# An FFT-style convolution on one core: steady tiles as two 64-row TensorE streams, and the last two frequencies inverted from on-chip memory

## The chip, the cores and the metric

The kernel runs on one core of a Trainium2 chip. The core has five engines that run side by side: TensorE (matmul), VectorE, ScalarE, GpSimd and SyncE, and 16 DMA engines. Operands lie in on-chip memory with 128 partitions; TensorE writes into eight accumulation banks (PSUM), from which VectorE and ScalarE read. The metric is the device time of one execution in microseconds. In the profile PE is TensorE's matmuls, PEld its weight loads, DVE is VectorE, ACT is ScalarE, POOL is GpSimd and SP is SyncE; a "q" behind a name is that engine's instruction queue.

## The reference

A circular 7 x 7 convolution of a 224 x 224 image with 96 channels in and 96 out, written with two-dimensional transforms:

```python
wp = jnp.pad(w, ((0, H - K), (0, W - K), (0, 0), (0, 0)))
Xf = rfft2(x, axes=(1, 2)); Wf = rfft2(wp, axes=(0, 1))
Yf = jnp.einsum('bhwi,hwio->bhwo', Xf, Wf)
y = irfft2(Yf, s=(H, W), axes=(1, 2)).astype(jnp.bfloat16)
```

Input and output are bf16; x is 1 x 224 x 224 x 96, w is 7 x 7 x 96 x 96.

## The kernel before

The kernel transforms only along the image's height, in eight bands of 28 output rows (with 6 rows more, a length of 34, so 17 frequencies s = 0 to 16). Along the width it uses the seven taps directly, with a fast scheme that computes two neighbouring columns at once: three products per pair (m = 0, 1, 2, with 4, 4 and 3 taps; `TAPS`). A complex product takes three real ones (three "parts"). For s > 0 that is 3 x 4 + 3 + 4 matmuls into a first bank and 2 x (3 + 4) into a second, 33 in all, and 22 for s = 0. Each has 96 rows of contraction (the channels), 128 columns of weights (16 column pairs by 8 bands) and 96 moving columns (output channels).

The width is cut into seven tiles of 32 columns (t = 0 to 6). A tile has these stages:

- A (`a_jobs`, line 395): forward transform; TensorE multiplies x, loaded into the four `xn` buffers, by the table `Fm`; ScalarE or VectorE moves the banks into `xf`. `evac` (line 115) gives each bank to the engine with the smaller running cost.
- J (`jit`, line 418): VectorE makes sums and differences of `xf` for groups of three frequencies (`JGB`), three instructions each, a burst that is handed to `b_round` as `planes`.
- B (`b_round`, line 446): the 33 matmuls against the transformed weights `WF`. ScalarE scales one part, VectorE forms u and v, and the sum u + v goes to `yf`: by GpSimd, or by VectorE (`ydve`) in a round that carries a burst.
- Frequencies go out of `yf` to a scratch buffer in DRAM (`scr`), three at a time (`YGRP`), and come back transposed as `tt` (`load_t`, line 537).
- C (`c_jobs`, line 568): inverse transform with the table `Gm` over three groups of bands, 24 matmuls of 384 columns a tile, moved to `yo` and out.

The order of each engine's instructions is that in which the program issues them[...]. Two tiles are worked first, t = 0 with t = 1 four rounds behind (`LAG`), while the weight transform (`prep_jobs`) is woven in; A of tile 2 runs in the last four rounds. Then tiles 2 to 6 follow one another. In each, A of the next tile and C of the two tiles before are woven between the rounds by `pace`. All loads and stores, but for a few at the end, are issued by SyncE in program order, each with its waits. The last tile writes its frequencies in three parts (0 to 8, 9 to 14, 15 and 16) to scratch; at the end the inverse adds one matmul with `GA` (the first part) and one with `GB` (the rest) per bank, and 36 matmuls on a zero tile (`WARM`) stand between them.

The profile names almost every operation by the one line of a helper (L84), so groups are told apart by tiles and shapes.

## Time and profile before

| | |
|---|---|
| time, three runs | 298.6, 299.13 (median), 299.9 us |
| span of the profiled execution | 298.6 us |
| what lies outside its span, against the median | 0.5 us |
| mean granted TensorE clock | 0.964 |
| busy: PE, PEld, DVE, ACT, POOL | 271.7, 243.5, 237.5, 197.8, 87.0 us |
| DMA moved | 46.01 MB, mean 154 GB/s |
| one B matmul (PE, mean) | 207 ns |
| one sum on GpSimd, on VectorE (mean) | 1006, 586 ns |

A matmul's 207 ns is from its start to its modelled end; they overlap, so PE counts as busy when one is under way, and the rate is read from starts. The chain is the sequence of work that ended last, followed back from the last instruction. A window's row gives, for a stretch of the span, the busy time and number of instructions of each engine, the granted clock (1.00 is full), the share of the DMA engines and their rate.

### The profile page before, as it was taken

What the parts mean: (1) busy time and instruction counts of PE and PEld (TensorE: products, weight loads), DVE (VectorE), ACT (ScalarE), POOL (GpSimd) and SP (SyncE); (2) the same over time, 40 slices, a digit from 0 to 9 for tenths busy, and PEclk for the clock granted to TensorE, in tenths of its full rate; (3) what the DMA queues carried; (4) which work ended last, traced back from release to release, by engine and by line L of the source; (5) the groups of instructions that cost most, each with busy time, mean ns of one, the idle gap of its engine ahead of it and who ended that gap; (6) DMA issues with size and microseconds to landing.
All of it is one profiled execution on the core that took longest, in us unless ns stands there. A gap on an engine that the chain in (4) does not pass through costs nothing.

```text
span 298.6 us, 11728 instructions
## 1 busy us (share of the span) xinstructions
PE 271.7 (91%) x4882; PEld 243.5 (82%) x4882; DVE 237.5 (80%) x508; ACT 197.8 (66%) x494; POOL 87.0 (29%) x124
## 2 busy tenths in 40 slices
PE   8488998988888886999999999999999999999992
PEld 3377987978887776989889989798998989788961
DVE  7846399999999948686988879876998889867823
ACT  2445995746452484888578886888789875676313
POOL 6810011222224421234152233234143223342100
PEclk9955999999999998999999999999999999999999
DMA  8894142111111357977847686687828643778765
GB/s 185 141 223 123 49 114 77 44 42 42 43 43 42 111 169 174 213 221 202 233 119 203 195 238 190 195 229 202 240 76 208 203 139 116 197 177 232 201 131 184
DMA packets 45828, 46.01 MB, mean 154 GB/s; under 512 B 33626, under 2 KB 34758, under 8 KB 45678
## 3 DMA queue, kind: packets, MB, share of 16 engines
q1 hardware_dynamic: 43488, 43.21, 54.3%
q10 hardware_dynamic: 2288, 2.06, 2.4%
q8 instruction: 38, 0.62, 0.9%
q14 instruction: 14, 0.11, 0.1%
HBM read 23.92 MB, written 21.33 MB: 152 GB/s over the span
## 4 chain that ended last, share of the span: by engine, by line
PE 59%; DVE 22%; DMA 7%; ACT 5%; issue 4%; SPq 1%; DVEq 0%; ACTq 0%
PE pb L84 59%; DVE J L84 7%; DVE v L84 5%; DMA wq<-in_w_dram 4%; DVE yf L84 3%; ACT WF L84 3%; DVE u L84 2%; DVE WF L84 2%; DVE xf L84 2%; DMA xf<-scrb 1%; ACT xf L84 1%; DMA xn<-in_x_dram 1%; SPq L84 1%; DMA scrb<-yf 1%; ACT yo L84 0%
## 5 line engine op out<-in xcount | busy, mean ns | idle before, releaser
L84 PE MATMUL pb<-WF,J 96*128 96x96 bf16 x2898 | 169.3, 207 | 7.9 <-DVE J L84 7.9
L84 PEld LDWEIGHTS <-J 96*128 96x128 bf16 (+1 forms) x2910 | 143.5, 98 | 24.2 <-DVE J L84 9.1
L84 POOL TENSOR_TENSOR yf<-v,u 128x384 bf16<-128x384 f32 x74 | 73.8, 1006 | 177.7 <-issue 103.2
L84 ACT CAST xf<-pb 96x408 bf16<-96x408 f32 (+1 forms) x153 | 67.3, 485 | 12.9 <-PE pb L84 10.1
L84 ACT CAST yo<-pb 84x384 bf16<-84x384 f32 (+1 forms) x144 | 61.3, 480 | 7.1 <-PE pb L84 4.1
L84 PE MATMUL pb<-WF,xf 96*128 96x96 bf16 x952 | 61.2, 207 | 4.4 <-DVE WF L84 4.3
L84 DVE TENSOR_TENSOR J<-xf 96x1824 bf16<-96x1824 bf16 (+1 forms) x84 | 57.4, 722 | 0.0
L84 PEld LDWEIGHTS <-xf 96*128 96x128 bf16 x952 | 47.8, 98 | 5.0 <-issue 4.2
L84 PE MATMUL pb<-Fm,xn 118*128 118x136 bf16 x448 | 50.0, 232 | 2.1 <-DVE u L84 1.5
L84 PE MATMUL pb<-tt,Gm 102*84 102x384 bf16 (+1 forms) x144 | 36.2, 329 | 1.1 <-DVE u L84 0.5
L84 ACT CAST WF<-pb 96x480 bf16<-96x480 f32 (+1 forms) x65 | 32.8, 587 | 6.0 <-PE pb L84 5.9
L84 PEld LDWEIGHTS <-xn 118*128 118x128 bf16 x448 | 31.8, 102 | 3.8 <-issue 2.9
L84 PE MATMUL pb<-wq 98*128 98x120 bf16 (+1 forms) x336 | 26.6, 232 | 3.5 <-DMA wq<-in_w_dram 3.5
L84 PEld LDWEIGHTS <-wq 98*128 98x128 bf16 (+1 forms) x336 | 23.6, 151 | 4.9 <-POOL ct L84 3.6
L84 DVE TENSOR_TENSOR J<-J 96x912 bf16<-96x912 bf16 (+1 forms) x42 | 25.0, 595 | 0.0
L84 DVE TENSOR_TENSOR yf<-v,u 128x384 bf16<-128x384 f32 x38 | 22.2, 586 | 1.3
L84 DVE TENSOR_TENSOR WF<-WF 96x480 bf16<-96x480 bf16 x30 | 18.7, 629 | 2.9 <-ACT WF L84 2.8
L84 PEld LDWEIGHTS <-Gm 102*84 102x84 bf16 (+1 forms) x144 | 11.5, 114 | 3.5 <-issue 0.8
L84 PE MATMUL pb<-wu 128*112 128x384 bf16 (+1 forms) x60 | 12.7, 374 | 1.1 <-DVE ct L84 1.1
L84 PEld LDWEIGHTS <-wu 128*112 128x112 bf16 (+1 forms) x60 | 7.3, 123 | 6.0 <-issue 2.1
L84 DVE CAST xf<-pb 96x408 bf16<-96x408 f32 (+1 forms) x19 | 8.9, 512 | 1.3 <-PE pb L84 1.3
L84 ACT CAST tt<-pb 112x384 bf16<-112x384 f32 x8 | 3.6, 479 | 9.2 <-PE pb L84 9.1
(388 smaller groups left out, 207.6 us busy)
## 6 DMA issues: line engine op xcount, KB each, us to landing
xn<-in_x_dram SPq DMA_DIRECT2D x28, 336.0 KB
scr<-yf SPq DMA_DIRECT2D x30, 288.0 KB
tt<-scr SPq DMA_DIRECT2D x24, 288.0 KB
out_dram<-yo SPq DMA_DIRECT2D x24, 252.0 KB
tt<-scr SPq DMA_DIRECT2D x12, 192.0 KB
out_dram<-yo SPq DMA_DIRECT2D x12, 168.0 KB
out_dram<-tt SPq DMA_DIRECT2D x4, 336.0 KB
scr<-yf SPq DMA_DIRECT2D x6, 192.0 KB
```

The costliest lines, as they stand in the source:

```text
L84: r = fn(*a, **k)
```

## The change

In tiles 2 to 6 the 96 channels no longer fill one 96-row matmul. TensorE's rows are used as two halves of 64, by `tile_position`. The lower half ("lo") takes channels 0 to 63, one matmul per tap. The upper half ("hi") holds channels 64 to 95 twice, the second time shifted by two taps, so one matmul does two taps; it also takes two of the three parts of m = 0 for channels 0 to 63, so that both halves have 25 or 26 matmuls a frequency. `t_round` issues them in turn, hi some 20 matmuls behind (`step8`, `FLUSH`); both add into the same bank, and before a bank's first hi matmul `row_wait` holds TensorE's queue until the last lo matmul is done. A (`f_jobs`) and C are split into 64-row halves in the same way; C now spans four bands with 512 columns, and frequency 16 goes through a small table `GR`.

The layout is made by copies on chip: `shift` copies channels 64 to 95 of `xf` to partitions 96 to 127 once per tile, `bring` copies channels 0 to 63 to partitions 64 to 127 per group of three frequencies, and `convert` rearranges `WF` once, group by group as tile 1 leaves it. All three are issued by SyncE. The weight transform's taps are put in the order of `TPOS` by ten small GpSimd copies. From tile 2 on all sums but the last three of tile 6 run on GpSimd and no longer wait for the burst; the halo copy of `xf` moves from VectorE to GpSimd. PSUM is split into 5 banks for B and 3 for the rest, `YBUF` goes from 4 to 3, and J keeps three buffers throughout. A of tile 2 is split: frequencies 0 to 7 four rounds earlier, the others in the last four rounds; its planes are made after the last round.

At the end frequencies 15 and 16 of the last tile stay in `yf`: `direct` adds them to the banks with 128 matmuls of 32 rows and 192 columns against the table `SG`, which `d_job` fills; `WARM` goes from 36 to 8, and the output goes in eight stores in place of four.

```diff
+TPOS = {7: 0, 8: 1, 2: 2, 0: 3, 1: 4, 3: 5, 9: 6, 6: 7, 4: 8, 5: 9}
...
+ND = 2 * (17 - 15)
 YMAX = 3
-YBUF = 4
+YBUF = 3
 JGB = ((0, 3), (3, 6), (6, 9), (9, 12), (12, 15), (15, 17))
 LAG = 4
-CQ = {2: (12, 0), 3: (12, 2), 4: (10, 5), 5: (7, 8), 6: (4, 12)}
-NXN = 4
-NP2 = 0
-WARM = 36
+CQ = {2: (6, 0), 3: (6, 0), 4: (6, 0), 5: (6, 0), 6: (6, 6)}
+SH = 8
+FLUSH = 20
+WARM = 8
...
+    def load_x(t, jg):
+        load_rows(xn_bufs[jg], jg, t * 2 * TW, 2 * PXC)
...
+    mo = ftile([PW2, NTAP])
+    for tap, pos in TPOS.items():
+        GE.tensor_copy(out=mo[:, pos:pos + 1], in_=mk[:, tap:tap + 1])
...
+    def d_job(a, g):
+        k = a * NJ + 4 * g
+        VE.tensor_tensor(out=SG[:, a, g].rearrange("p q (j m) -> p q j m", j=4), in0=Gv[:].unsqueeze(2).to_broadcast([128, ND, 4, B]),
+                         in1=Gk[:, k:k + 4].unsqueeze(1).unsqueeze(3).to_broadcast([128, ND, 4, B]), op=ALU.mult)
...
+                o, i = (v[0:C, ph, :, s0:s1, p:p + HALO, :].rearrange("c r s w j -> c r s (w j)") for v, p in ((xf, 0), (prev, TW)))
+                apart(("A", t), ("halo", s0), (VE if t < 2 else GE).tensor_copy(out=o, in_=i))
...
+    def f_jobs(t, part, jgs, tiled, load):
+        s0, s1 = ((0, SH), (SH, NS))[part]
+        n = 2 * (s1 - s0) * JG
+        runs = ((0, 8), (8, 16)) if part == 0 else ((0, 6), (6, 11), (11, 16))
+        fv = Fm[:, :, s0:s1].rearrange("p r s j -> p r (s j)")
+        jobs = []
+
+        def mk_(jg, a, b, last):
+            xb = xn_bufs[jg]
+            m = b - a
+            st = {}
+
+            def mm(ph, k, h, start=True, stop=True):
+                i = 2 * (a + k) + ph
+                p0, p1 = ((0, R), (0, 64), (64, R))[h]
+                kw = {} if h == 0 else dict(tile_position=(p0, 0), skip_group_check=True)
+                return TE.matmul(st["b"][ph][:, k * n:(k + 1) * n], lhsT=xb[p0:p1, i * C:i * C + 128], rhs=fv[p0:p1],
+                                 start=start, stop=stop, **kw)
+
+            def put():
+                for ph in range(2):
+                    xo = xf_tiles[t][0:C, ph, :, s0:s1, HALO + a:HALO + b, jg * JG:(jg + 1) * JG]
+                    pi = st["b"][ph][0:C, 0:m * n].rearrange("c (w r s j) -> c r s w j", r=2, s=s1 - s0, w=m)
+                    apart(("A", t), (a, jg, ph, part), evac(xo, pi, m * n))
+                if last and load:
+                    load_x(t + 1, jg)
+
+            def full():
+                st["b"] = [bank(), bank()]
+                for ph in range(2):
+                    for k in range(m):
+                        mm(ph, k, 0)
+                put()
+
+            def one():
+                st["b"] = [bank(), bank()]
+                for k in range(m):
+                    st["e"] = [mm(ph, k, 1 + ph, k == 0, False) for ph in range(2)]
+
+            def two():
+                row_wait(*st["e"])
+                for k in range(m):
+                    for ph in range(2):
+                        mm(ph, k, 2 - ph, False, True)
+                put()
+            return [one, two] if tiled else full
+        for jg in jgs:
+            for a, b in runs:
+                jobs.append(mk_(jg, a, b, b == 16))
+        return jobs
+
+    row_reg = []
+
+    def row_wait(*prev):
+        if not row_reg:
+            row_reg.extend(nc.alloc_registers("rows", engines=OrderedSet([mybir.EngineType.PE])))
+            TE.reg_mov(row_reg[0], 1)
+        w = TE.reg_mov(row_reg[0], row_reg[0])
+        for p in prev:
+            tc.add_manual_dep(w.ins, p.ins.name, SYNC, reason="row tiles of one bank")
+
+    def shift(t):
+        xf = xf_tiles[t].rearrange("c p r s w j -> c (p r) (s w j)")
+        dma(xf[C:128, :, 2 * NJ:], xf[64:C, :, 0:NS * PP - 2 * NJ])
+
     jbuf = {}
+    bbuf = {}
+    b_bufs = []
     jcount = [0]
+
+    def bring(t, g):
+        s0, s1 = JGB[g]
+        bb = b_bufs[(t * len(JGB) + g) % 2]
+        dma(bb[64:128, :, 0:s1 - s0].rearrange("c r s q -> c r (s q)"),
+            xf_tiles[t][0:64, 0, :, s0:s1].rearrange("c r s w j -> c r (s w j)"))
+        for s in range(s0, s1):
+            bbuf[(t, s)] = bb[:, :, s - s0]
...
-        xf = xf_tiles[t][0:C]
-        xv = xf.rearrange("c p r s w j -> c p r s (w j)")
-        b = jcount[0] % 3 if t < 2 else (jcount[0] - 2 * len(JGB)) % 2
+        rows = C if t < 2 else 128
+        xv = xf_tiles[t][0:rows].rearrange("c p r s w j -> c p r s (w j)")
+        b = jcount[0] % 3
...
+    def put_y(t, s, ycur):
+        yf, y0, y1 = ycur
+        if t == TL and s >= SB:
+            ylast.append(yf[:, s - y0])
+        elif s == y1 - 1:
+            dst, yo0, ye = scr_tiles[t], 0, min(y1, NS - 1)
+            if t == TL:
+                i = int(s >= SA)
+                dst, yo0 = scr_tiles[(t, i)], (0, SA)[i]
+            dma(dst.rearrange("w j s e -> (w j) s e")[:, y0 - yo0:ye - yo0], yf[:, 0:ye - y0].rearrange("p s r m o -> p s (r m o)"))
+            if y1 == NS:
+                dma(scr_tiles[(t, "r")].rearrange("w j e -> (w j) e"), yf[:, NS - 1 - y0].rearrange("p r m o -> p (r m o)"))
...
-                if last is not None:
+                if last is not None and t < 2:
                     tc.add_manual_dep(y.ins, last.ins.name, SYNC, reason="sum after planes")
...
+    def step8():
+        while pend and pend[0][0]:
+            pend.pop(0)[1]()
+        if pend:
+            pend.pop(0)[1]()
+        while pend and pend[0][0]:
+            pend.pop(0)[1]()
+
+    def t_round(t, s, job, ydve=False, planes=lambda: ()):
+        ycur = yslot(t, s)
+        pl = views(t, s, 128)
+        bb = bbuf[(t, s)]
+        bs = (bank("p"), bank("p"))
+        lo, hi = ([], []), ([], [])
+        ends = {}
+
+        def mm(h, g, i, src, k, sl, pos):
+            r0 = 64 * h
+            st = h == 0 and not lo[g]
+            first8 = h == 1 and not hi[g]
+
+            def f():
+                if first8:
+                    row_wait(ends[g])
+                r = TE.matmul(bs[g][:, i * C:(i + 1) * C], lhsT=src[r0:r0 + 64, (HALO - k) * NJ:(HALO - k) * NJ + 128],
+                              rhs=WF[r0:r0 + 64, sl, pos, :], start=st, stop=False, tile_position=(r0, 0), skip_group_check=True)
+                if h == 0:
+                    ends[g] = r
+            (lo, hi)[h][g].append((False, f))
+        for g, grp in enumerate(cols(s)):
+            for i, (m, part) in enumerate(grp):
+                src, sl = pl[part][m], slot(s, part)
+                moved = m == 0 and part > 0
+                for k, tap in enumerate(TAPS[m]):
+                    if not moved or (s % 2 and part == 2 and k == 3):
+                        mm(0, g, i, src, k, sl, TPOS[tap])
+        for g, grp in enumerate(cols(s)):
+            for i, (m, part) in enumerate(grp):
+                src, sl = pl[part][m], slot(s, part)
+                for k in range(2):
+                    mm(1, g, i, src, k, sl, TPOS[TAPS[m][k]])
+                if m == 0 and part > 0:
+                    for k in range(4):
+                        if not (s % 2 and part == 2 and k == 3):
+                            mm(1, g, i, bb[:, part % 2 if s else part], k, sl, 6 + k)
+        st = {}
+
+        def cba():
+            st["a"] = vec_a(s, bs[0])
+
+        def cbx():
+            st["x"] = vec_x(s, bs[0], st["a"])
+
+        def cby():
+            vec_y(t, s, bs[1], *st["x"], ydve, planes(), ycur)
+        job = list(job)
+
+        def hook():
+            if job:
+                job.pop(0)()
+        for i, (_, f) in enumerate(lo[0]):
+            if i == 3:
+                hook()
+            f()
+            step8()
+        hook()
+        na = len(hi[0]) - (0 if s == 0 else 4)
+        pend.extend(hi[0][:na] + [(True, cba)] + hi[0][na:] + [(True, cbx)])
+        for i, (_, f) in enumerate(lo[1]):
+            if i == 9:
+                hook()
+            f()
+            step8()
+        pend.extend(hi[1] + [(True, cby)])
+        while sum(not c for c, _ in pend) > FLUSH:
+            step8()
+        assert not job
+
+    def drain():
+        while pend:
+            step8()
+
+    ylast = []
+    def convert(gi):
+        s0, s1 = PGRP[gi]
+        a, b = slot(s0, 0), slot(s1 - 1, 2) + 1
+        W = WF.rearrange("i a t o -> i a (t o)")
+        for d, q, n in ((0, 6, 2), (2, 7, 2), (4, 9, 1)):
+            dma(W[C:128, a:b, d * C:(d + n) * C], W[64:C, a:b, q * C:(q + n) * C])
+        for d, q in ((6, 0), (8, 6)):
+            if s0 == 0:
+                dma(W[64:128, 1, d * C:(d + 2) * C], W[0:64, 1, q * C:(q + 2) * C])
+                a = 2
+            for p in (1, 2):
+                dma(W[64:128, a + p:b:3, d * C:(d + 2) * C], W[0:64, a + p:b:3, 
...
+            def mk_(q, h=h, hold=hold):
+                st = {}
+
+                def mm(g, src, gm, r0, start):
+                    st[g] = TE.matmul(st["b"][g][0:4 * B, :], lhsT=gm[r0:r0 + 64, :],
+                                  rhs=src[r0:r0 + 64].rearrange("p w e -> p (w e)")[:, q * 512:(q + 1) * 512],
+                                  start=start, stop=False, tile_position=(r0, 0), skip_group_check=True)
+
+                def one():
+                    if q == 0:
+                        hold["yo"] = [yo_pool.tile([4 * B, PXC * C], BF16, name="yo") for _ in range(2)]
+                    st["b"] = [bank(), bank()]
+                    for g in range(2):
+                        mm(g, tt_tiles[(t, h)][0][g], G, 64 * g, True)
+
+                def two():
+                    row_wait(st[0], st[1])
+                    for g in range(2):
+                        mm(g, tt_tiles[(t, h)][0][g], G, 64 - 64 * g, False)
+
+                def three():
+                    row_wait(st[0], st[1])
+                    for g in range(2):
+                        mm(g, tt_tiles[(t, h)][1], GR[:, h], 64 * g, False)
+                    for g in range(2):
+                        evac(hold["yo"][g][:, q * 512:(q + 1) * 512], st["b"][g][0:4 * B, :], 512)
+                    if q == 2:
+                        w0 = t * 2 * TW + h * PXC
+                        for g in range(2):
+                            dma(out[0, g * 4 * B:(g + 1) * 4 * B, w0:w0 + PXC, :].rearrange("h w c -> h (w c)"), hold["yo"][g][:])
+                        held[0] -= 1
+                        pump()
...
+        if r == NS - 4:
+            new_xf(2, 0, SH)
+            add(2 * r, 2 * NS, f_jobs(2, 0, (0, 1), False, False))
         if r == NS:
-            add(2 * r, 2 * (r + LAG) - 2, a_jobs(2))
+            new_xf(2, SH, NS)
+            add(2 * r, 2 * (r + LAG) - 2, f_jobs(2, 1, (0, 1), False, True) + [lambda: shift(2)])
+        if 5 <= r < 10:
+            GE.memset(WF[C:128, (r - 5) * 10:(r - 4) * 10, 5, :], 0.0)
...
+            if t == 1:
+                for gi, (s0, s1) in enumerate(PGRP):
+                    if s == s1 - 1:
+                        convert(gi)
...
+    pools["p"] = ctx.enter_context(tc.tile_pool(name="psp", bufs=5, space=bass.MemoryType.PSUM))
+    pools["j"] = ctx.enter_context(tc.tile_pool(name="psj", bufs=3, space=bass.MemoryType.PSUM))
...
+    for g in range(2):
+        bring(2, g)
+        for f in jit(2, g):
+            f()
...
+            fj = [f_jobs(t + 1, p, (jg,), True, p == 1 and t + 2 < NT) for jg in range(2) for p in range(2)]
+            for s, j in enumerate(sum(fj, [])):
+                jobs[s + 1] = j
...
+        for u, g, r in [(t, g, JGB[g][0]) for g in range(2, len(JGB))] + [(t + 1, 0, NS), (t + 1, 1, NS + 3)]:
+            if u < NT:
+                plan.setdefault(r - 5 + (u > t and g == 0), []).append(("j", u, g))
+                plan.setdefault(r - 4 + (u > t and g == 0), []).append(("b", u, g))
...
+            if s == 11 and t + 1 < NT:
+                shift(t + 1)
...
+    def direct(g, qs_):
+        for a in range(4):
+            for i in range(ND):
+                for q in qs_:
+                    if q % 2 == a // 2:
+                        k = q // 2 * 32
+                        TE.matmul(live[(g, q)][:, a % 2 * 2 * C:(a % 2 + 1) * 2 * C], lhsT=SG[k:k + 32, a, g, i],
+                                  rhs=ylast[i // 2][k:k + 32, i % 2].rearrange("p m o -> p (m o)"),
+                                  start=False, stop=False, tile_position=(k, 0))
...
+    direct(0, range(8))
...
+            if g == 1 and q % 4 == 0:
+                direct(1, range(q, q + 4))
```

## Prediction

> **What bounds the kernel now.** I read the shares by engine and the chain first, then a table of windows cut at the tiles, the chain in order of time, and the timeline at three places.

> ```profile
> PE 271.7 (91%) x4882; PEld 243.5 (82%) x4882; DVE 237.5 (80%) x508; ACT 197.8 (66%) x494; POOL 87.0 (29%) x124
> ...
> PE 59%; DVE 22%; DMA 7%; ACT 5%; issue 4%; SPq 1%; DVEq 0%; ACTq 0%
> ```

> TensorE is most of the chain. The windows (busy us of PE, PEld, DVE, ACT, POOL; clock; DMA share, GB/s) show where:

> ```profile
> 104.00:116.00 12.00, 8.12 (x164) 7.77 (x164) 7.01 (x16) 8.59 (x24) 2.41 (x4) 1.00 0.60 173
> 116.00:151.00 35.00, 35.00 (x672) 32.32 (x669) 28.30 (x61) 25.79 (x66) 10.33 (x11) 0.95 0.89 213
> 151.00:185.00 34.00, 33.28 (x646) 30.14 (x643) 28.48 (x59) 26.94 (x69) 11.24 (x12) 1.00 0.66 188
> 185.00:219.00 34.00, 33.67 (x650) 30.21 (x647) 28.19 (x59) 27.55 (x71) 10.99 (x12) 1.00 0.72 204
> ```

> ```profile
> 188.69 70.22 PE pb L84 x1345
> ...
> 282.82 1.96 DMA scrb<-yf
> 284.85 4.22 DMA xf<-scrb
> 289.12 3.78 PE pb L84 x21
> ```

> Tiles 2 to 6 run from 115.6 to 281 us with TensorE never idle for long (one link of 70 us). Before that lies a hand-over (104 to 116) in which no engine is full; after it, a trip through DRAM for the last frequencies.

> ```profile
> 109.99 0.76 PE L84 MATMUL pb<-WF,J 96*128 96x96 bf16 x14
> ...
> 114.46 1.40 DVE L84 TENSOR_TENSOR J<-xf 96x1824 bf16<-96x1824 bf16 x2
> ...
> 115.61 0.56 PE L84 MATMUL pb<-WF,J 96*128 96x96 bf16 x9 [2.35 <-DVE J L84]
> ```

> One conv matmul is 207 ns long, so 14 of them start every (760-207)/13 = 42.5 ns. The other steps, from the starts in the trace: A matmuls 59 ns, inverse matmuls 162 ns. A tile is 550 conv + 64 A + 24 inverse = 23.3 + 3.8 + 3.9 = 31.0 us; five tiles, the last without A and with six inverses in all, 155 us. They take 165.4, so 10.3 us are unfilled, 1.7 of it clock: after the 2.35 us gap above the clock falls to half for some 3.4 us.

> ```profile
> 116.00:118.00 2.00, 2.00 (x34) 2.00 (x31) 2.00 (x5) 0.49 (x1) 0.00 (x0) 0.62 0.69 171
> 118.00:120.00 2.00, 2.00 (x23) 1.78 (x21) 2.00 (x5) 0.91 (x3) 0.00 (x0) 0.53 1.32 202
> ```

> [...] The trace of before has no row tiles: it shows 42.5 ns for 96 columns, weight loads starting 2 ns after a matmul, and at closest 15 ns from load to load, so four instructions in 42.5 ns are possible but not shown. [...] two J differences take 1.40 us alone (above), and with a sum running on GpSimd:

> ```profile
> 251.94 1.98 DVE L84 TENSOR_TENSOR J<-xf 96x1824 bf16<-96x1824 bf16 x2
> ```

> **The change, part by part.**

> *Conv of tiles 2 to 6.* 33 matmuls per frequency become 51 of 64 rows: 25 or 26 for channels 0 to 63 (lo) and 26 or 25 for the rest (hi), issued in turn. Per tile 426 pairs (16 x 25.5 + 18). If a pair costs one stream's step, 426 x 42.5 = 18.1 us against 23.3.

> *A stage.* 64 matmuls of 136 columns become 256 of 64 or 72, 128 pairs. By the slope (59-42.5)/40 = 0.41 ns a column a pair is 31 ns, so 4.0 us against 3.8: no gain. *Inverse:* 18 pairs of 512 columns at 216 ns (as the 512-column warm-up), 3.9 against 3.9.

> So a tile falls from 31.0 to 26.0 us, and the five with their six inverses from 155 to 130.

> *Row waits.* Before a second stream enters a bank TensorE's queue waits for the first: two per frequency, one per A job, two per inverse job, about 56 per tile. All later matmuls queue behind. In the order of instructions the awaited matmul lies some 8 pairs (340 ns) back and needs 207 ns, so most of it is covered; I take 20 ns each, 1 us per tile. Bounds: 0, and 100 ns each, 28 us in all.

> *VectorE and ScalarE.* From starts back to back: u 268, v 461 ns (16 each), J bursts 5 x 1.87 + 1.31 us; 22.8 us per tile. Six sums and the halo copies leave it for GpSimd (6 x 0.48 + 1.4 us less), and the wait that kept sums off the bursts is dropped: each burst may lose up to 1 us to a sum, 0 to 6 us per tile. Up to 26 us this hides behind TensorE, so I count nothing; without that cover it is up to 3 us per tile. ScalarE takes every evacuation: 16 x 0.31 + 12 x 0.47 + 20 x 0.42 = 19 us. Hidden too.

> *On-chip copies.* Per tile one shift (32 partitions, 657 KB) and six "bring" copies (662 KB). [...] DMA now moves 6.4 to 6.9 MB per tile (188 and 204 GB/s by 34 us) at a share of about 0.7; 1.32 MB more fits. In steady tiles the shift has three rounds (about 5 us) before its planes are due: hidden, just. On SP everything waits in order, so a late bring stops the hi stream.

> *Hand-over to tile 2.* Here the cover is missing. A jobs in the last four rounds are halved (half ran earlier), and the wait for x at 109.8 us goes; four rounds of 33 x 42.5 ns (5.6 us) and 64 matmuls of 72 columns (2.7 us, if no faster than 42.5 ns) end 8.3 us after 103.7, where these rounds begin; ten small GpSimd copies ahead of the weight transform at the start add 1 us: 113. Then SP holds, in order: shift, two puts that wait for the last GpSimd sum (about 115), seven weight moves, four of which wait for three to land (2 us), at 0.35 us an issue, then bring. It lands near 122; the hi stream needs it. Tile 2 starts at 121.5 instead of 115.6, 6 us lost (bounds 2 and 10). The clock drop stays 1.7 us.

> *Buffers.* Conv keeps 5 PSUM banks, two a round, the other work 3: TensorE may run one round (1.5 us) ahead of VectorE, then it stops. I count nothing while VectorE has time to spare.

> *Weight moves, memsets, tables* run on idle queues or GpSimd time between 20 and 100 us, except as counted.

> *Tail.* The DRAM trip of frequencies 15 and 16 (1.96 + 4.22 us) goes, and 28 warm-up matmuls with it; 128 matmuls of 32 rows and 192 columns come, 82 ns each by the slope: 2.6 us if four run side by side, 10.5 in a row, half of it ahead of each half of the output rows. I take 6, so the tail stays 16.4 us (282.2 to 298.6); bounds 13 and 21.

> *Sum on the profiled execution:* 121.5 + 130 + unfilled 8.6 (as before, without the clock) + clock 1.7 + row waits 5 + tail 16.4 = 283.2. A pair will hardly be quite 42.5 ns; each ns costs 5 x 426 + 4 x 128 = 2640 pairs x 1 ns = 2.6 us, and I add 0.7 ns: **285 us**. The profiled 298.6 is 0.5 below the median of 299.13; the forecast stays 285.

> **Rivals.**

> *The queue is the limit (slower).* Lo and hi are issued alternately by one in-order queue. [...] If instructions come no faster than now (two in 42.5 ns), a pair is 85 ns: 395, and the change does not do what it says. For it: before never issues a matmul under 41 ns after another. Against: loads start 2 ns after a matmul. It decides above 48 ns a pair (15.4 / 2.64 = 5.8 ns more).

> *The gain turns into waits on copies[...].* Pairs cost 43 ns, but a late shift stalls VectorE and bring stops the hi stream, or sums take bursts: 2.5 us a tile, 12.5 us: 297, about no change. For it: 0.58 us lost in the one collision shown, SP strictly in order, DMA share already up to 0.89. Against: VectorE has 3 us to spare per tile.

> **How the numbers follow.** Overlap works and TensorE stays the bound: 0.50, with a range of 273 to 296. Waits on copies[...]: 0.17, 289 to 303. Queue limit: 0.33, 300 to 395, most of it below 330. A measurement of this kernel can tell 0.5% (1.5 us) from no change. Faster: 0.50 x 0.95 + 0.17 x 0.6 = 0.57; same 0.07; slower 0.36. The range of 270 to 325 leaves out 0.03 below and 0.14 above.

> **What would show it.** Conv matmuls of 64 rows in twos 42 ns apart, tile starts (the sum of frequency 0 on VectorE) 28 to 29 us apart, a gap of about 8 us before tile 2 ended by a bring or the shift, VectorE at 22 to 26 us per tile. Wrong if pairs start over 48 ns apart, if gaps before conv name DMA or J in the steady tiles, or if TensorE's own queue ends them (row waits).

## The result and the profile after

| | before | after |
|---|---|---|
| time, median (lowest to highest) | 299.51 (298.6 to 303.09) us | 459.21 (452.91 to 463.05) us |
| ratio, 95% interval | | 1.522 [1.507, 1.537] |
| span of the profiled execution | 298.6 us | 451.2 us |
| mean granted TensorE clock | 0.964 | 0.823 |
| DMA moved | 46.01 MB | 55.70 MB |

The kernel is slower by half; the forecast was 285 us with a range of 270 to 325. The page's shares by engine and its chain (the chain breaks off a few matmuls before the end and tells nothing here):

```profile
PE 293.2 (65%) x7386; PEld 250.7 (56%) x7386; DVE 248.2 (55%) x481; ACT 175.2 (39%) x403; POOL 164.3 (36%) x220
...
PE 3%; issue 0%; ACT 0%; DVE 0%; DVEq 0%; ACTq 0%
```

TensorE was 91% busy and is now 65%: no engine is full. The windows, cut at the hand-over and at tiles 2 to 4 (busy us of PE, PEld, DVE, ACT, POOL; clock; DMA share, GB/s):

```profile
117.00:145.00 28.00, 6.72 (x148) 5.86 (x145) 7.87 (x16) 2.82 (x8) 4.92 (x5) 0.63 0.68 168
145.00:202.00 57.00, 36.96 (x1140) 31.49 (x1138) 29.55 (x51) 21.43 (x49) 19.39 (x16) 0.79 0.51 130
202.00:257.00 55.00, 33.19 (x1155) 28.21 (x1151) 29.36 (x51) 21.33 (x49) 21.76 (x18) 0.91 0.54 140
257.00:315.00 58.00, 37.52 (x1147) 31.61 (x1142) 29.84 (x52) 21.33 (x49) 22.64 (x19) 0.77 0.51 136
```

A tile takes 54 to 58 us where it took 32 to 35. By the start of the sum of frequency 0 in each tile, the 152.6 us of span are lost so: 10.6 before tile 0 (42.6 for 32.0), 17.5 from there to tile 2 (102.3 for 84.9), 89.6 in tiles 2 to 5 (224.2 for 134.6), and 34.9 in tile 6 with the tail (82.0 for 47.1).

The two streams do what they should. Three places of the timeline at the start of tile 3 (start, duration, engine, operation, count, idle time before it and who ended it):

```profile
200.63 0.56 PE L86 MATMUL pb<-WF,J 64*128 64x96 bf16 x18
...
201.47 0.43 PE L86 MATMUL pb<-Fm,xn 64*128 64x64 bf16 x16
...
202.84 0.24 PE L86 MATMUL pb<-WF,J 64*128 64x96 bf16 x2
...
203.46 0.42 ACT L86 ACTIVATE tt__4411<-pb 128x288 f32<-128x288 f32 x1
203.93 0.26 PE L86 MATMUL pb<-WF,J 64*128 64x96 bf16 x4 [0.85 <-ACT tt__4411 L86]
```

Eighteen matmuls in 0.56 us, each 0.20 long, are (560-200)/17 = 21 ns apart: 42 ns a pair. The transform's sixteen are (430-200)/15 = 15 ns apart, 31 ns a pair. At 202.84 TensorE starts two more and then nothing until 203.93, when ScalarE has scaled the first bank (`tt__`). That is the first loss. The waits over the whole run (engine waiting and who ended it: us, times, longest) show the others:

```profile
PE pb L86 <- DMA rb<-scrr: 34.2, 7, 6.4
...
DVE J L86 <- DMA xf<-xf: 13.2, 1, 13.2
...
ACT tt__592 L86 <- POOL GR L86: 10.1, 1, 10.1
```

In tile 3, of 54.9 us, start-to-start gaps over 150 ns that end in the scaling are 17.2 us (16 of them), the one that ends in the reload of `rb` (frequency 16 for the inverse) 5.4, those in which nothing is waited for that the profile shows ("issue") 7.0, a bring 0.7. Of the 7.0, 4.4 are the inverse's own steps, each after a matmul of 512 columns, and 2.6 lie at two places that the end of the next section explains. So 29.0 us are the matmuls themselves, at a mean clock of 0.91, where 26.0 were forecast at full clock. The hand-over, on the timeline:

```profile
118.82 7.92 SPq L86 DMA_DIRECT2D WF<-WF  x7
...
128.31 0.65 SPq L86 DMA_DIRECT2D xf<-xf  x1
...
131.89 8.32 SPq L86 DMA_DIRECT2D WF<-WF  x7
136.25 1.42 DVE L86 TENSOR_TENSOR J<-xf 128x1824 bf16<-128x1824 bf16 x2 [13.23 <-DMA xf<-xf]
...
137.42 0.26 PE L86 MATMUL pb<-WF,J 64*128 64x96 bf16 x1 [14.00 <-DVE J L86]
...
140.30 1.24 SPq L86 DMA_DIRECT2D bb<-xf  x2
...
142.61 0.26 PE L86 MATMUL pb<-WF,bb 64*128 64x96 bf16 x1 [4.59 <-DMA bb<-xf]
```

The shift stands behind one group of weight moves, bring behind the next, each 8 us of SyncE's time; TensorE stops for 14.0 and again for 4.6 us.

### The profile page after: what moved, and what is told of

It is laid out like the page before. It is cut to its first block, busy times and chain, and to the rows that moved or that the text cites. A ratio compares the mean times of both kernels' runs of the same rounds, so it can differ in the third digit from the quotient of the medians.

```text
span 451.2 us, 16780 instructions
## 1 busy us (share of the span) xinstructions
PE 293.2 (65%) x7386; PEld 250.7 (56%) x7386; DVE 248.2 (55%) x481; ACT 175.2 (39%) x403; POOL 164.3 (36%) x220
## 2 busy tenths in 40 slices
DMA packets 59265, 55.70 MB, mean 123 GB/s; under 512 B 42891, under 2 KB 49399, under 8 KB 59095
## 5 line engine op out<-in xcount | busy, mean ns | idle before, releaser
L86 PE MATMUL pb<-WF,J 64*128 64x96 bf16 (+1 forms) x4058 | 212.0, 218 | 92.7 <-DVE J L86 18.7
L86 PEld LDWEIGHTS <-J 64*128 64x128 bf16 (+2 forms) x4070 | 176.7, 104 | 115.8 <-issue 89.4
L86 POOL TENSOR_TENSOR yf<-v,u 128x384 bf16<-128x384 f32 x99 | 120.9, 1223 | 255.5 <-DVE v L86 183.5
L86 DVE TENSOR_TENSOR J<-xf 128x1824 bf16<-128x1824 bf16 (+3 forms) x84 | 80.4, 998 | 13.2 <-DMA xf<-xf 13.2
L86 ACT CAST xf<-pb 96x512 bf16<-96x512 f32 (+4 forms) x133 | 61.3, 536 | 63.4 <-PE pb L86 63.4
L86 PE MATMUL pb<-WF,xf 64*128 64x96 bf16 (+1 forms) x672 | 82.2, 218 | 2.8 <-DVE WF L86 2.0
L86 PE MATMUL pb<-Fm,xn 64*128 64x72 bf16 (+6 forms) x1280 | 55.1, 207 | 15.3 <-ACT tt__592 L86 6.9
L86 PEld LDWEIGHTS <-xn 54*128 54x128 bf16 (+4 forms) x1440 | 50.9, 105 | 19.5 <-issue 13.1
L86 PE MATMUL pb<-WF,bb 64*128 64x96 bf16 x620 | 57.7, 222 | 5.9 <-DMA bb<-xf 5.1
L86 PEld LDWEIGHTS <-xf 64*128 64x128 bf16 (+1 forms) x672 | 48.9, 105 | 13.4 <-issue 6.8
L86 PE MATMUL pb<-rb,GR 64*112 64x512 bf16 x72 | 19.6, 508 | 34.2 <-DMA rb<-scrr 34.2
L86 DVE TENSOR_TENSOR WF<-WF 96x480 bf16<-96x480 bf16 x30 | 17.1, 579 | 12.5 <-ACT WF L86 12.4
```

The source lines that it names most:

```text
L86: r = fn(*a, **k)
```

## The experiments

Every edit is to the changed kernel, alone or on top of those named. The first four take one wait away each; their theory is that the wait costs what its gaps show, and the rival that something else is late next.

**The scaling after the bank's last matmul** (`e1_scale_last`). The program put it before the last four hi matmuls of the first bank. These write columns 288 to 479, ScalarE reads 0 to 287, yet they wait for it (0.85 us at 203.93 above), so the wait seems to be kept for the bank as a whole; by what, the trace does not show.

```diff
-        na = len(hi[0]) - (0 if s == 0 else 4)
+        na = len(hi[0])
```

> The changed kernel with one difference: ScalarE's scaling of a frequency's first bank is issued after the bank's last matmul, not four matmuls before it. Theory: those last four matmuls write the bank that ScalarE is reading, so TensorE's queue stands still from the third-last part's end until ScalarE is done, once per frequency; the profile after has 83 such gaps of about 1.05 us, 17 us per tile, 87 us in all. They go, the tiles are about 40 us apart in place of 56, and the time is about 372 us (360 to 385). Rival: the gap only shows where TensorE has to wait for a slow ScalarE or VectorE, and the wait moves to the next bank or to the sums: less than 30 us gained, over 420 us.

Measured: 416.27 us (413.63 to 418.92), ratio 1.384 [1.363, 1.405]. All the scaling gaps are gone, and half of their 87 us came back. The waits of this kernel show where the other half went:

```profile
PE pb L86 <- DMA rb<-scrr: 44.1, 7, 7.8
...
PEld L86 <- DMA bb<-xf: 16.8, 5, 5.1
```

The rb wait rose from 34.2 to 44.1 us, bring is late three times more, and the stalls without a releaser that last over 0.6 us rose from 8.1 to 21.0 us. Tiles take 47 to 51 us, at a clock of 0.79 to 0.82 in three of them.

**One reload of rb per tile** (`e2_rest_reload`). Both halves of a tile shared one buffer, each with a load of its own, so the second half's first matmul waited for a load that could start only when the first half was done.

```diff
-        rb = r_bufs[0]
-        dma(rb[4 * h:128:8], ...)
+    def load_r(t):        # both halves, issued after the tile's last inverse job
```

> The changed kernel with one difference: the buffer of frequency 16 is loaded once per tile, after the second half's last inverse matmul, not in halves between the two. Theory: the one buffer serves both halves, so the second half's first use waits for a load that belongs to the next tile; the profile after has seven such waits, 34 us in all. Once per tile is then early enough, but for the last tile, where two inverses follow each other (one wait of some 5 us stays): about 430 us (424 to 438). Rival: these waits lie in the shadow of ScalarE's (the scaling waits), and no more than 10 us go: over 445 us.

Measured: 416.62 us (413.1 to 420.14); 42.6 gained, more than the waits themselves. They are gone but for the last tile, and tiles 2 to 5 ran at a clock of 0.92 to 0.96 instead of 0.77 to 0.91 (over the whole span its two runs had 0.871 and 0.899, the kernel after 0.808 to 0.823): with the gap of some 5 us a tile the drop of the clock behind it goes too, which fits the rest of the gain.

**The tables' scratch in memory of its own** (`e3_tables_kept`): an idle J buffer instead of the temporary memory in which the first scaling's buffer is placed.

```diff
-        ... gr = ftile([128, 4, B])
+        q, fl, gr = (J_bufs[1][:, i * 256:...].bitcast(F32)... for i in range(3))
```

> The changed kernel with one difference: the scratch of the small GpSimd tables is not in the temporary memory that the first rounds' buffers take over, but in an idle plane buffer. Theory: the first scaling of tile 0 waited 10.1 us for GpSimd's last table because its buffer reuses that memory; the first sum of frequency 0 comes at about 32 us as before, in place of 42.6, and the time falls by 8 to 10 us to about 448. Rival: the first rounds wait for the weight transform anyhow, and under 3 us are gained.

Measured: 449.47 us (448.99 to 449.95). Tile 0 starts at 35.3 instead of 42.6 us, so this is the cause of 7.3 us of the late start; the kernel before starts it at 32.0, and the other 3.3 us were not looked into.

**Two groups of weight moves later** (`e4_weights_later`):

```diff
-                    if s == s1 - 1:
+                    if s == s1 - 1 and gi < 4:
                         convert(gi)
...
+    convert(4)
+    convert(5)     # after the shift, two brings and the first J of tile 2
```

> The changed kernel with one difference: the last two groups of weight copies are issued after the shift and the first two brings of tile 2. Theory: SyncE is in order, and each group holds it for about 8 us (7 issues of 0.6 us and a wait of 3 us for the first three to land), so the shift was issued at 128.3 and the first bring at 140.3 us though their data were ready at 121; the hand-over shrinks by 10 to 14 us, from 21 us between the last matmul of tile 1 and the first sum of tile 2 to about 9, and the time is about 447 us. Rival: the shift's own transfer is the length of the gap (it landed 8 us after its issue), and under 5 us are gained.

Measured: 452.63 us (452.5 to 452.77). From tile 1 to tile 2 it is 72.5 us for 82.6, the 10 us that the order on SyncE cost. Of the whole time little came back: the ratio is 1.505 [1.501, 1.509] against 1.522 [1.507, 1.537], not told apart, and the profiled runs are equally long (451.1 and 451.2 us). Tile 2 then waits 6.4 us for a bring, and tiles 2 to 5 take 56 to 60 us where they took 54 to 58.

**All four together** (`e5_all_four`), and **sums after the bursts** on top (`e6_sum_after`), which gives tiles 2 to 6 back the rule that a GpSimd sum waits until VectorE's J burst is done:

```diff
-                if last is not None and t < 2:
+                if last is not None:
```

> The four single differences together: scaling after the bank's last matmul, frequency 16 reloaded once per tile, table scratch kept out of the temporary memory, last weight groups after the shift and the brings. Theory: the waits were one behind the other on TensorE's in-order queue[...], so the sum of the parts is exceeded: start 8, hand-over 10, per tile 17 + 5 and the clock; tiles about 36 us apart, 325 us (305 to 345). That is still slower than before, since short waits between the two streams and late brings stay. Rival: the waits only uncover another bound (VectorE held up by GpSimd's sums, 29 us busy per tile), tiles stay above 43 us: over 360 us. Second rival: with the waits gone the two streams bring the whole gain that was forecast: under 295 us.

> As the kernel with all four differences, and GpSimd's sum waits for the burst of plane differences on VectorE in tiles 2 to 6 too, as it does in the first two tiles. Theory: [...]a plane burst has been up to 2 us longer (VectorE's plane differences 80 us in all after, 57 before), but VectorE is not what TensorE waits for, so the bursts get shorter by some 20 us in all and the time by less than 5 us. Rival: VectorE is the bound once the waits are gone: 15 us or more are gained.

Measured: 377.03 us (376.18 to 380.1), ratio 1.254 [1.246, 1.263], and 373.51 us (365.46 to 376.87), 1.241 [1.226, 1.255]: by their intervals the two can't be told apart, though the fastest run of the second is 11 us below the fastest of the first. What a GpSimd sum beside the burst costs VectorE is plain in the kernel after, whose groups by shape in tiles 2 to 5 (count, busy us, mean ns) have

```profile
L86 DVE TENSOR_TENSOR J<-xf 128x456 bf16<-128x456 bf16 x20 | 23.8, 1192 | 0.0
```

where the kernel before has

```profile
L84 DVE TENSOR_TENSOR J<-xf 96x456 bf16<-96x456 bf16 x20 | 7.7, 384 | 0.0
```

so 0.8 us in each of six bursts, where the expectation has up to 2, and nearly 5 us a tile. The rule takes it away, as `e6_sum_after` shows for the same shape:

```profile
L86 DVE TENSOR_TENSOR J<-xf 128x456 bf16<-128x456 bf16 x20 | 7.8, 389 | 0.0
```

Between the medians this gave 3.5 us; the 15 us or more that would have made VectorE the bound did not come. Here the first theory falls: the waits that I could name (some 130 us) add up to far more than the 82 us that the kernel gave back, and tiles still take 40 to 47 us with TensorE idle for a quarter of the time.

**Lo and hi in blocks** (`e7_in_blocks`, on the four): the hi matmuls are no longer woven between the lo ones.

```diff
             f()
-            step8()
```

> As the kernel with all four differences, but the two streams are not issued in turn: a frequency's 25 lo matmuls come first, then its hi matmuls, so that neighbours in the queue belong to the same half. The same instructions. Theory: two halves run at once only if their matmuls stand next to each other; a frequency's 51 matmuls then take 51 x 42.5 ns in place of 26, 18 us more per tile, 70 to 90 us in all. Rival (queue limit): the queue's rate decides, order does not matter, and the time is the same within 10 us.

Measured: 476.73 us (472.83 to 480.63), 100 us slower than woven, some 23 us a tile (67.8 for 44.5). The windows of two tiles hold a surprise:

```profile
150.00:217.00 67.00, 64.30 (x1116) 59.87 (x1112) 28.44 (x50) 21.62 (x48) 22.23 (x18) 0.58 0.43 114
217.00:284.00 67.00, 64.70 (x1135) 60.80 (x1134) 28.90 (x51) 21.74 (x48) 21.66 (x19) 0.58 0.43 114
```

TensorE is busy for 64 of 67 us and yet granted a clock of 0.58 (0.69 and 0.724 over the two runs, 0.833 to 0.888 woven). So the 23 us hold two things, the lost overlap and the clock, and are not divided here. That the overlap itself is lost shows in the steps, first at full clock, then at half:

```profile
191.15 0.76 PE L86 MATMUL pb<-WF,J 64*128 64x96 bf16 x14
...
151.47 1.06 PE L86 MATMUL pb<-WF,J 64*128 64x96 bf16 x11
```

That is (760-200)/13 = 43 ns a matmul, where woven a pair takes 42, and some 80 ns at half clock.

**What is left: where the gaps without a releaser lie.** In the improved kernels the long gaps marked "issue" all come at places in TensorE's stream that are a whole number of 256 instructions apart, counted over all its records: in `e6_sum_after` 21 of 21 that last over 0.6 us after the first 60 us, in the kernel after 6 of 6; the kernel before has none, and neither has `e7_in_blocks`, where the same instructions go by more slowly (7.2 us for 256, median). The DMA queues show packets of instructions that fit such blocks. The kernel after has 58 in 0.95 MB, 16.4 KB each, for 7,386 matmuls and as many weight loads, 255 to a packet, and `e8_bring_rb` has as many (packets, MB, share):

```profile
q8 instruction: 58, 0.95, 1.2%
```

The kernel before has 38, for 4,882 of each: 257 to a packet. Five more kernels follow, each built on `e6_sum_after`; the padded ones test whether the stalls belong to these blocks, the one with less traffic whether other transfers hold the packets up.

**Bring on ScalarE's queue (but for the first two of tile 2), and a place of its own for the last tile's rb** (`e8_bring_rb`):

```diff
-        dma(bb[64:128, :, 0:s1 - s0]...
+        (SE.dma_start if t > 2 or g > 1 else dma)(bb[64:128, :, 0:s1 - s0]...
...
+    r_bufs.append(xn_all[:, o + 12 * B:o + 12 * B + TW * C]...)   # used for t == TL - 1
```

> Built on the kernel in which the four waits are taken away and the GpSimd sum follows the plane subtractions (373.5 us). Two things more: the on-chip copy of the even rows (bring) is issued on ScalarE's queue instead of SyncE's, where it stood behind puts that wait for GpSimd, and the last tile's one-frequency table has its own place, so that its load need not wait for the half before it. Theory A, these waits add up: the bb gaps of tiles 3 to 6 (about 12 us in all) and the last tile's rb gaps (11 us) go, TensorE's clock is a little better, 350 us (345 to 358). Theory B, TensorE's instructions come in blocks of 256 and a block takes 3.3 to 4 us to come: what is no longer waited for elsewhere is waited for at the block borders instead, the gaps without a releaser grow from 27 us in all to 32 or more, and the time falls by 12 us or less, to about 362.

Measured: 365.95 us (360.18 to 371.15), ratio 1.204 [1.190, 1.218], 7.6 us less than the median of the step before; the fastest runs, 360.18 and 365.46, are 5.3 apart. The bb gaps of tiles 3 to 6 fell from 12 to 4 us, rb from 11 to 6; the stalls at block borders rose from 28.1 to 32.6 us. That is theory B, with the reserve that `e5_all_four` already had 31.1. One of them on the timeline:

```profile
225.78 0.25 PE L86 MATMUL pb<-WF,J 64*128 64x96 bf16 x3
228.77 0.27 PE L86 MATMUL pb<-WF,J 64*128 64x96 bf16 x2 [2.74 <-issue]
```

The border before it was at 223.40; the packet that brings the next block starts at 225.94 and ends at 227.20; the first matmul of the block starts at 228.77. From 120 us on, the median from a border to the start of the next packet is 1.8 us and the packet takes 1.2; where TensorE stalls, the first instruction follows 1.4 us after the packet's end. Between borders lie 4.83 us (median; 3.45 at the 5th percentile), while 256 instructions at four per 42.5 ns would be gone in 2.7. In the kernel before, 256 instructions last 6.5 us, and the packet for the next ones has landed some 5 us ahead (if its borders lie at the same places of the stream; no stall marks them). A steady tile has some 2,300 instructions, nine blocks. In tiles 2 to 5 of `e8_bring_rb` the gaps of over 150 ns at borders sum to 6.2 to 9.8 us a tile, where the kernel after has 1.3 to 2.7; 2.4 to 3.7 us more end in a move of the inverse out of its banks, and up to 2.0 in a bring. Without the border gaps such a tile would take some 34 us (an estimate: 42.6 less 8.2, the means), as in the kernel before.

**The first shift in two parts** (`e9_early_shift`, on `e8_bring_rb`):

```diff
-            add(2 * r, 2 * NS, f_jobs(2, 0, (0, 1), False, False))
+            add(2 * r, 2 * NS, f_jobs(2, 0, (0, 1), False, False) + [lambda: shift(2, 0, SH)])
...
-            add(2 * r, 2 * (r + LAG) - 2, f_jobs(2, 1, (0, 1), False, True) + [lambda: shift(2)])
+            add(2 * r, 2 * (r + LAG) - 2, f_jobs(2, 1, (0, 1), False, True) + [lambda: shift(2, SH, NS)])
```

> The kernel with bring on ScalarE and the own table place, and the first shift sent in two parts: frequencies 0 to 7 as soon as their transform is done (four rounds earlier), the rest where it was. If the hand-over is bound by that shift (the 8 us gap on J before tile 2): tile 2 starts 5 to 9 us earlier, and the time falls by as much. Rival: the 35 weight moves and the puts on SyncE hold it up anyway, or TensorE then waits for the even rows (bb) of tile 2 instead: tile 2 starts as before or starts earlier and stops at its first matmul on bb, under 2 us in all.

Measured: 369.72 us (365.04 to 374.4), no gain; from tile 1 to tile 2 it took 77.2 us for 71.2. The waits name the new one: ScalarE's copies into the rest of `xf` now wait for the first part of the shift, which reads the same buffer.

```profile
ACT xf L86 <- DMA xf<-xf: 7.2, 1, 7.2
```

**Padding** (`e10_padded`, on `e9_early_shift`; then `e11_64_more`, on `e8_bring_rb`).

```diff
+    for _ in range(128):
+        TE.reg_mov(row_reg[0], row_reg[0])            # e10_padded
...
+    for _ in range(32):
+        TE.matmul(pwu[:, 0:64], lhsT=wu[:, 0:128], rhs=wu[:, 0:64], start=True, stop=True)   # e11_64_more
```

> The early-shift kernel with 128 register moves put into TensorE's stream at the hand-over, where TensorE waits in any case. [...] If the gaps without a releaser are those of instruction blocks of 256, they come 128 instructions of the program away from where they were: counted in the trace without the moves, their place modulo 256 changes from 194 to 66, all of them. If they belong to certain matmuls (a bank, a row wait, a transform), they stay at the same matmuls, at 194. The time stays within 1% of the kernel without the moves.

> The kernel with bring on ScalarE, with 32 dummy matmuls (64 instructions with their weight loads) more at the hand-over, into a bank that nobody reads; the register moves of the padded kernel turned out not to be in the compiled stream. If the stalls belong to the 256-instruction blocks in which TensorE's stream arrives, they stay at places that are 194 modulo 256 counted over all records, and so come 64 instructions of the program earlier, at other matmuls; 58 or 59 instruction packets of 16 KB are seen. If they belong to certain matmuls, their place becomes 2 modulo 256 (194 + 64). The time is that of the kernel without them within 2%.

The first told nothing. It has as many records of TensorE as `e9_early_shift` (14,837), and the borders lie 256 records apart although the program's register moves are not among them, so these do not seem to be in the compiled stream. It repeats `e9_early_shift` (371.54 us, 368.5 to 375.52; places at 194). The second, one run of 359.54 us: all 20 long stalls lie at 194 modulo 256 counted with the 64 added instructions, so at other matmuls than before. They belong to the block, not to a bank or a row wait.

**Less traffic** (`e12_less_dma`, on `e8_bring_rb`), with part of the loads left out:

```diff
     def load_t(t, h):
+        if t > 0:
+            tt_tiles[(t, h)] = (tt_tiles[(0, h)][0], r_bufs[t == TL - 1])
+            return
...
     def load_x(t, jg):
+        if t > 3:
+            return
```

> The kernel with bring on ScalarE (366 us), with part of the work left out: from tile 4 on the transform uses the rows of tile 3 again, and every inverse but the first tile's uses the first tile's rows again, so 0.7 MB of x loads and 1.5 MB of tt loads a tile are not moved, and the output is that of other data; the instructions of TensorE are the same in number and order. Theory A, the packet that brings TensorE's next 256 instructions stands behind data packets: with less traffic the time from a block border to that packet falls from 1.7 us (median) to 1.1 or less, a block's period from 4.8 to about 3.8 us, tiles 3 to 5 from 42 to 36 us or less, 340 us in all. Theory B, the packet's delay is its own and does not depend on this traffic: periods stay at 4.6 to 4.9 us and tiles at 40 us or more; only waits for tt go, under 6 us in all.

Measured: 343.61 us (341.21 to 348.36), ratio 1.143 [1.134, 1.151]. The windows of tiles 3 and 4, here at full clock:

```profile
161.00:198.00 37.00, 28.94 (x1120) 25.23 (x1114) 23.86 (x50) 21.65 (x49) 18.26 (x18) 1.00 0.42 117
198.00:236.00 38.00, 29.71 (x1142) 25.94 (x1142) 24.92 (x52) 22.05 (x49) 18.32 (x18) 1.00 0.42 121
```

From a border to the packet it is 1.2 us instead of 1.8 (medians), a block lasts 4.39 us instead of 4.83, tiles 38 to 42 us. So traffic does delay the packet, and most of the delay stays without it. Yet the stalls of over 0.6 us at borders sum to 34.2 us, no less than the 32.6 with all the traffic. The 22 us came from elsewhere: 10 in the last tile with the tail, the rest in tiles 2 to 5, three of which ran at full clock. In tiles 3 and 4 the gaps of over 150 ns at borders are 7.5 and 9.0 us; what is left after all gaps but the inverse's own steps is 26.3 and 26.0 us, about what the sum gave (26.0). Without its border gaps such a tile would take some 30 us (an estimate from the same numbers); a tile of the kernel before takes 32 to 35. No kernel here came near the kernel before.

## Why the prediction was wrong

- *A pair costs one stream's step*: right, though no trace had shown two row halves at once. 42 ns a pair in tile 3, transform pairs 31 ns, as forecast. At full clock the matmuls of a tile need what the sum gave them, 26.0 and 26.3 us in `e12_less_dma`.
- *"ScalarE takes every evacuation: 19 us. Hidden too."*: the step that failed first and most. Its busy time was right (21 us a tile), but it was weighed as a sum. Where the program puts the scaling in TensorE's order decides: before a bank's last four matmuls, it makes TensorE wait about 1.05 us in each of 16 rounds, 17 us a tile and 87 in all, of which `e1_scale_last` got 43 back. I had read `na` as a detail and asked only whether the engine had time, not who waits for it.
- *Buffers, "I count nothing"*: `rb` alone, one buffer with two loads a tile, costs 34.2 us by the waits and slowed the clock besides (0.77 to 0.91 in tiles 2 to 5, 0.92 to 0.96 in `e2_rest_reload`).
- *Row waits, 1 us a tile*: not seen to cost more. In tiles 2 to 5 of the kernel after, 70 of the 71 gaps of over 0.1 us without a releaser and away from block borders stand next to a matmul of the inverse, whose steps the sum holds already (the kernel before has 111 such gaps). Shorter waits were not measured.
- *Hand-over, tile 2 starts at 121.5*: TensorE stood still until 137.4 and again until 142.6; 10.6 us of that is the late start of tile 0, the next point. I counted 0.35 us an issue and 2 us of waiting for seven weight moves; a group holds SyncE for 8 us, and two groups lie in the way, one ahead of the shift. The shift itself took 8 us from its issue to VectorE's start; that three rounds (about 5 us) hide it was my estimate, with no trace behind it.
- *Weight moves, memsets, tables "on idle queues or GpSimd time"*: the table of frequency 16 runs when nothing else does, but its scratch lies where the first scaling writes: 7 us of late start, by `e3_tables_kept`.
- *Unfilled time 8.6 us and 1.7 us for the clock, "as before"*: the new gaps brought new clock drops. After each of the eight gaps of over 4 us behind the first 60 us of the kernel after, the clock is at half; other stretches at half clock come without such a gap. The mean clock of the run fell from 0.964 to 0.823.
- *VectorE*: 29 us a tile by the windows where 22.8, and up to 6 for sums beside the bursts, were counted; hidden, as said.
- *The rival "the queue is the limit"* was tested against the wrong sign. I looked for pairs further apart than 48 ns and they are not (a matmul every 21 ns in tile 3, every 15 in the transform); its lower end, 300 us, was my estimate, which no trace had shown. A limit sits in the supply: averaged over a block, its other waits included, `e8_bring_rb` gets 4 instructions per 4.83/64 = 75 ns, and 54 in the quickest twentieth. I did not count instructions: 1,144 matmuls a tile in place of 638, each with a weight load, make nearly twice as many in a time meant to shrink. In the kernel after, this costs only 1.3 to 2.7 us a tile, hidden behind the other waits; in `e8_bring_rb` it is 6 to 10, much of what the removal of the others did not bring.
- *The tail, 16.4 us*: from the last convolution matmul to the end it is 15.8 us, where the kernel before takes 17.7, so a little better than forecast and within its bounds.

What stays open: what delays the instruction packet after a border (1.2 us even with the traffic cut), why the clock stays low when lo and hi come in blocks, and how the losses that remain in the last tile of `e8_bring_rb` (67.5 us with the tail, for 47.1) divide between block borders, `rb` and the banks of the inverse.

## What to carry to other kernels

Before splitting matmuls into smaller concurrent ones, count instructions: here a block of 256 of TensorE's lasted 3.5 to 5 us where four per 42 ns would use it up in 2.7, so that rate was not sustained, though each burst ran at it. Weigh an engine not by its busy time but by where its result is waited for in TensorE's order: here a reader of a bank, placed ahead of that bank's last matmuls, stopped everything behind them for about 1.05 us, 16 times a tile. And when several waits lie in one stream, take them away together in one experiment before adding up their gaps: four that showed some 130 us gave 82.
